# Decode attention over two key/value caches on one core: blocks of 8192 keys by 8 heads, 16 KB runs per load, output weights loaded last

## The chip, the core and the metric

The kernel runs on one core of a Trainium2 chip. The metric is the device time of one execution in microseconds (us), the median of several. The engines' short names in the profile are PE (TensorE; PEld its weight loads), DVE (VectorE), ACT (ScalarE), POOL (GpSimd) and SP (SyncE, which here issues the loads). "DMA engines" are the sixteen engines that move data between HBM and SBUF.

## The reference

Two attention blocks decode one token each. Block A has 32 heads over 32,768 keys, each head with its own cache. Block B has 32 query heads on 8 cache heads and looks only at the last 4096 keys. Everything is bfloat16, head size 128, model width 512.

```python
# A: q = x @ wq -> (1, 32, 1, 128)
scores = jnp.einsum("bhqd,bhkd->bhqk", q, k_cache) * (Dh ** -0.5)
p = _softmax(scores, axis=-1)
o = jnp.einsum("bhqk,bhkd->bhqd", p, v_cache)
out_A = o.transpose(0, 2, 1, 3).reshape(B, Sq, H * Dh) @ wo
# B: the same over k_cache[:, :, Sk-4096:, :], each of 8 cache heads serving 4 query heads
# result: concatenate([out_A, out_B], axis=-1)
```

Both caches are read once: 536.9 MB for A and 16.8 MB for B, and 16.8 MB of weights. That is 570.4 MB in all. Each byte of A's K and V is used for one query only, each byte of B's for four.

## The kernel before

The kernel works in rounds of 2048 keys by all 32 heads (two rounds of B, 16 of A). A load brings 2048 keys of two heads (1 MB). A partition holds 16 neighbouring keys of 128 bfloat16, which is a run of 4 KB in HBM.

```python
ROWS = 2048
def kv_src2(self, name, which, r, kvh0):
    base = d["key0"] + ROWS * r
    ap = d[which][0, kvh0:kvh0 + 2, base:base + ROWS, :]
    return ap.rearrange("s (p j) d -> p s j d", j=JT)          # JT = 16: 4 KB runs
```

In a round, PE transposes each K tile (into PSUM, DVE copies it back), and multiplies it with a query column, so that the scores of all 32 heads end in 128 partitions of one PSUM bank. The softmax follows over the whole bank. The probabilities are then "spread": 32 small matmuls with a 0/1 matrix place them so that they can serve as PE weights, and ACT copies each product back. Only then can the PV matmuls of that round run, while K of the next round arrives:

```python
for uu, unit in enumerate(kunits):                 # 16 K units of a round
    ...                                            # transposes and scores of two heads
    if s == 0 and uu >= self.SPREAD_POS and spreads:
        emit_spreads(j, spreads[:4], sp_first)     # 4 of 32 per unit
    if uu + 1 >= self.PVSTART and not spreads and vi < len(vunits):   # PVSTART = 9
        emit_PV(j, vunits[vi], vi == 0)            # one V unit per K unit
        vi += 1
...
while vi < len(vunits):                            # what is left, in one go
    emit_PV(j, vunits[vi], vi == 0)
```

With eight V buffers and PV starting at the ninth unit, eight of the 16 PV units are left for the round's end. The last loads of the kernel are the output weights of A, in 1 KB runs, and then 16 V units. (The code above is shortened.)

## Time and profile before

The median before was 1474.56 us (1472.97 to 1483.99, 3 runs).

| what | value |
|---|---|
| busy PE / DVE / ACT | 77% / 50% / 21% |
| load queue, share of sixteen engines' time | 98.1% |
| mean rate of HBM reads | 387 GB/s |

These lines come from the page of the kernel before: busy time of the engines, the stretch of 40 slices (DMA in tenths, GB/s), the DMA packets, the load queue (q1), the queue that fetches instructions (q8), and the chain of work that ended last.

```profile
PE 1135.4 (77%) x15670; PEld 774.8 (53%) x15670; DVE 732.5 (50%) x1240; ACT 307.2 (21%) x601; POOL 6.1 (0%) x25
...
DMA  9999999999999999999999999999999999999994
GB/s 353 392 395 403 387 390 409 392 409 408 393 408 375 409 373 408 401 389 358 389 409 373 409 406 377 409 379 408 373 409 396 395 403 392 407 391 409 386 394 160
DMA packets 157360, 572.64 MB, mean 388 GB/s; under 512 B 9761, under 2 KB 17953, under 8 KB 157218
...
q1 hardware_dynamic: 157218, 570.46, 98.1%
q8 instruction: 123, 2.02, 0.6%
...
DMA 51%; PE 33%; SPq 9%; ACT 4%; DVE 1%; issue 1%; ACTq 0%; DVEq 0%
```

A "98.1%" queue looks like a bound that nothing but fewer bytes could move. But the slices swing between 358 and 409 GB/s. The windows view of the kernel before (columns: stretch, its length, then busy time and instruction count of each engine, granted clock of PE, DMA share, GB/s) tells three states apart:

```profile
core 0: us, PE busy (x) PEld busy (x) DVE busy (x) ACT busy (x) POOL busy (x), PEclk, DMA share, GB/s
22.00:24.00 2.00, 0.00 (x0) 0.00 (x0) 0.00 (x0) 0.00 (x0) 0.00 (x0) 1.00 1.06 390
435.00:440.00 5.00, 4.38 (x79) 3.10 (x77) 3.44 (x6) 0.00 (x0) 0.00 (x0) 0.98 1.03 410
455.00:460.00 5.00, 5.00 (x146) 4.37 (x144) 1.16 (x2) 0.00 (x0) 0.00 (x0) 0.93 0.54 167
1405.00:1410.00 5.00, 3.18 (x6) 0.52 (x6) 0.50 (x4) 3.55 (x8) 0.00 (x0) 0.50 1.10 352
1452.00:1454.00 2.00, 1.11 (x16) 0.63 (x16) 0.00 (x0) 0.00 (x0) 0.00 (x0) 0.50 0.40 154
1454.00:1456.00 2.00, 0.92 (x16) 0.63 (x16) 0.00 (x0) 0.00 (x0) 0.00 (x0) 0.50 0.03 12
```

Query weights in 2 KB runs stream at 390 GB/s (row 22), K and V in 4 KB runs at 410 (row 435), output weights in 1 KB runs at 352 (row 1405), each with a DMA share at or above 1. Row 455 is a gap: PE is busy for all 5 us with 146 matmuls, and the engines carry 167 GB/s at a share of 0.54. From about 1453 on nothing moves, and the kernel ends at 1475.3. Who held the loads back is told by the waits of the load queue (L361 is line 361 of the kernel; columns: us waited in total, times, longest):

```profile
SPq L361 <- PE psACC L504: 650.9, 126, 18.3
SPq L352 <- PE psT L432: 139.9, 74, 9.8
```

The loads of V (L361) waited 650.9 us in total for PV matmuls (L504) to set a buffer free. Most of those waits cost nothing, since other loads were in flight; row 455 shows where one did.

### The profile page before, as it was taken

The numbers are of one execution on the slowest core, as the hardware profiler recorded it, in microseconds if no ns is written. First come the engines' busy times: TensorE is split into PE (matmuls) and PEld (weight loads), VectorE is DVE, ScalarE is ACT, GpSimd is POOL, SyncE is SP. The second block draws the span as 40 slices with busy tenths as digits, with TensorE's granted clock in tenths as the row PEclk, the third lists the DMA queues.
The fourth block names the chain that finished last, engine by engine and source line by source line (L and its number), as shares of the span: only waits on it lengthen the run. The fifth ranks groups of instructions, "written<-read, shape, count | busy, mean of one in ns | idle before, by whom it ended". The sixth has DMA issues, their size and how long they took to land.

```text
span 1475.3 us, 34189 instructions
## 1 busy us (share of the span) xinstructions
PE 1135.4 (77%) x15670; PEld 774.8 (53%) x15670; DVE 732.5 (50%) x1240; ACT 307.2 (21%) x601; POOL 6.1 (0%) x25
## 2 busy tenths in 40 slices
PE   2989878687777878878787878777787787878764
PEld 2656565555555455555545555554555555555522
DVE  1567545455454545544454645545455554545403
ACT  0112204040311304031130403113040311304040
POOL 1000000000000000000000000000000000000000
PEclk9799989999998979897998989989899998989956
DMA  9999999999999999999999999999999999999994
GB/s 353 392 395 403 387 390 409 392 409 408 393 408 375 409 373 408 401 389 358 389 409 373 409 406 377 409 379 408 373 409 396 395 403 392 407 391 409 386 394 160
DMA packets 157360, 572.64 MB, mean 388 GB/s; under 512 B 9761, under 2 KB 17953, under 8 KB 157218
## 3 DMA queue, kind: packets, MB, share of 16 engines
q1 hardware_dynamic: 157218, 570.46, 98.1%
q8 instruction: 123, 2.02, 0.6%
q14 instruction: 19, 0.16, 0.0%
HBM read 570.43 MB, written 0.00 MB: 387 GB/s over the span
## 4 chain that ended last, share of the span: by engine, by line
DMA 51%; PE 33%; SPq 9%; ACT 4%; DVE 1%; issue 1%; ACTq 0%; DVEq 0%
DMA kbuf<-in_A_k_cache_dram 47%; PE psT L432 21%; SPq L361 6%; PE psS L455 5%; ACT ptz L849 4%; PE psP L481 3%; PE psACC L504 3%; DMA vbuf<-in_A_v_cache_dram 3%; SPq L352 2%; DMA kbuf<-in_B_k_cache_dram 1%; SPq L326 1%; SPq L341 1%; PE psP L410 0%; DVE kt L682 0%; PE psACC L613 0%
## 5 line engine op out<-in xcount | busy, mean ns | idle before, releaser
L682 DVE COPY kt<-psT 128x1024 bf16<-128x1024 bf16 x1056 | 687.5, 687 | 561.7 <-PE psT L432 553.1
L432 PE MATMUL psT<-ident,kbuf 128*128 128x128 bf16 x8448 | 629.0, 235 | 203.6 <-DMA kbuf<-in_A_k_cache_dram 172.7
L432 PEld LDWEIGHTS psT<-ident,kbuf 128*128 128x128 bf16 x8448 | 538.4, 106 | 328.8 <-DMA kbuf<-in_A_k_cache_dram 211.4
L849 ACT ACTIVATE ptz<-psP 128x512 bf16<-128x512 f32 x512 | 276.6, 594 | 341.6 <-PE psP L481 341.5
L481 PE MATMUL psP<-E_A,psb 32*128 32x512 bf16 x512 | 183.9, 401 | 75.3 <-ACT ptz L849 60.4
L455 PE MATMUL psS<-kt,qzA 128*32 128x512 bf16 x2048 | 214.1, 411 | 0.4 <-DVE kt L682 0.4
L504 PE MATMUL psACC<-vbuf,ptz 128*32 128x256 bf16 x4224 | 172.6, 297 | 47.7 <-DMA vbuf<-in_A_v_cache_dram 45.9
L504 PEld LDWEIGHTS psACC<-vbuf,ptz 128*32 128x32 bf16 x4224 | 143.6, 139 | 71.3 <-DMA vbuf<-in_A_v_cache_dram 53.2
L830 ACT ACTIVATE alpha_A<-m_A,nb 128x1 f32<-128x1 f32 x16 | 4.7, 294 | 702.0 <-DVE nb L694 702.0
L481 PEld LDWEIGHTS psP<-E_A,psb 32*128 32x128 bf16 x512 | 37.9, 92 | 213.2 <-ACT ptz L849 181.9
L455 PEld LDWEIGHTS psS<-kt,qzA 128*32 128x32 bf16 x2048 | 54.2, 94 | 58.6 <-DVE kt L682 13.2
L712 DVE SCALAR_TENSOR_TENSOR o_A<-o_A,alpha_A,psACC 128x256 f32<-128x256 f32 x16 | 7.7, 481 | 152.1 <-PE psACC L504 152.1
L852 ACT ACTIVATE ptz<-psP 128x288 bf16<-128x288 f32 x32 | 11.4, 408 | 24.4 <-PE psP L481 23.7
L690 DVE TENSOR_REDUCE cmax<-psS 128x1 f32<-128x512 f32 x18 | 12.5, 692 | 2.3 <-PE psS L455 0.5
L832 ACT ACTIVATE psb<-psS,nb 128x512 bf16<-128x512 f32 x18 | 12.0, 668 | 0.0
L830 ACT ACTIVATE alpha_B<-m_B,nb 128x1 f32<-128x1 f32 x2 | 0.6, 294 | 52.1 <-DVE nb L694 52.1
L481 PE MATMUL psP<-E_B,psb 32*128 32x288 bf16 x32 | 8.0, 289 | 3.2 <-ACT ptz L852 3.1
L455 PE MATMUL psS<-kt,qzB 128*32 128x512 bf16 x64 | 6.8, 438 | 1.1 <-DVE kt L682 0.8
L481 PEld LDWEIGHTS psP<-E_B,psb 32*128 32x128 bf16 x32 | 2.3, 91 | 9.2 <-ACT ptz L852 7.2
L863 ACT ACTIVATE e_gamma_A<-m_A,e_nb_A 128x1 f32<-128x1 f32 x1 | 0.3, 295 | 31.3 <-DVE e_nb_A L771 31.3
L807 DVE COPY e_part_A<-psACC 1x512 f32<-1x512 f32 x4 | 2.7, 686 | 3.4 <-PE psACC L613 3.4
L644 DVE COPY E_A<-ident 32x16 bf16<-32x16 bf16 x4 | 0.8, 195 | 7.1 <-POOL out_sb L314 7.0
(106 smaller groups left out, 70.3 us busy)
## 6 DMA issues: line engine op xcount, KB each, us to landing
kbuf<-in_A_k_cache_dram SPq DMA_DIRECT2D x256, 1024.0 KB, 12.7
vbuf<-in_A_v_cache_dram SPq DMA_DIRECT2D x256, 1024.0 KB, 13.1
kbuf<-in_B_k_cache_dram SPq DMA_DIRECT2D x8, 1024.0 KB, 13.9
vbuf<-in_B_v_cache_dram SPq DMA_DIRECT2D x8, 1024.0 KB, 13.0
vbuf<-in_B_wq_dram SPq DMA_DIRECT2D x4, 1024.0 KB, 8.8
vbuf<-in_A_wq_dram SPq DMA_DIRECT2D x4, 1024.0 KB, 14.5
wob<-in_B_wo_dram SPq DMA_DIRECT2D x4, 1024.0 KB, 13.7
kbuf<-in_A_wo_dram SPq DMA_DIRECT2D x4, 1024.0 KB, 12.0
```

The lines of the kernel that those rows point to most:

```text
L326: e.dma_start(self.wq_view(ch), src).then_inc(self.vfull[slot], 16)
L341: e.dma_start(self.wo_view(ch), src).then_inc(sem, 16)
L352: e.dma_start(self.K_buf[slot][:, :, :, :], src).then_inc(self.kfull[slot], 16)
L361: e.dma_start(self.V_buf[slot][:, :, :, :], src).then_inc(self.vfull[slot], 16)
L432: inst = t.transpose(self.T[tb][:, 128 * jjj:128 * (jjj + 1)], self.K_buf[kslot][:, s, j, :], self.ident[:, :])
L455: inst = t.matmul(self.S[sb_][32 * c:32 * c + 32, :], lhsT=win, rhs=self.KT[ktslot][:, 512 * c:512 * (c + 1)], start=(hh == 0), stop=(hh = ...
L481: inst = t.matmul(out_ap, lhsT=lhsT, rhs=rhs, start=True, stop=True, tile_position=(32 * c, 0))
L504: inst = t.matmul(self.ACC[32 * c:32 * c + 32, 0:2 * DH], lhsT=self.pt_window_unit(name, c, jj, win_u), rhs=self.V_buf[vslot][:, 0:2, tile ...
L682: inst = v.tensor_copy(self.KT[ktslot][:, 1024 * half:1024 * (half + 1)], self.T[tb][:, :])
L690: seq(v.reduce_max(self.cmax[:, :], self.S[j % 2][:, :], axis=AXX))
L832: s.activation(out=self.p_sb[j % 2][:, :], in_=self.S[j % 2][:, :], func=ACTF.Exp, bias=self.nb[:, :], scale=self.SCALE, accum_out=self.ro ...
L849: inst = s.activation(out=tz[:, 512 * half:512 * (half + 1)], in_=self.P[pb][:, 0:512], func=ACTF.Copy)
```

## The change

The intent is to keep the DMA engines streaming in long runs. The kernel is rewritten; this is a shortened cut of the diff, with comments in place of what is left out:

```diff
-ROWS = 2048
-        ap = d[which][0, kvh0:kvh0 + 2, base:base + ROWS, :]
-        return ap.rearrange("s (p j) d -> p s j d", j=JT)
+        a["KC"], b["KC"] = 4, 2
+            d["HG"] = 32 // d["KC"]                # 8 heads of A at a time, 16 of B
+            d["blk"] = 2048 * d["KC"]              # 8192 keys of A, 4096 of B
+        ap = d[which][0, h0:h0 + nh, base:base + d["blk"], :]
+        return ap.rearrange("s (p j) d -> p s (j d)", p=128)   # 16 KB runs (A), 8 KB (B)
 ...
-        # 32 spreading matmuls and 32 ACT copies per round
+        for jj in range(4):                        # probabilities transposed whole
+            inst = e.transpose(PT[:, 128*jj:128*jj+128], pb[:, 128*jj:128*jj+128], ident)
+        # one ACT copy per round
 ...
+                    if i > 0 and pr == 1 and u % 2 == 1 and pv_done < dp["nvu"]:
+                        self.emit_PV(i - 1, pv_done)   # one 4 MB V unit after every 2nd K unit
 ...
-        src = X[name]["wo"][1024*k:1024*(k+1), :].rearrange("(a p) c -> p a c", p=128)
+        src = self.X[name]["wo"].rearrange("(p a) c -> p (a c)", a=32)   # 32 KB a row
+            if u == d["nvu"] - 1:                  # after the last V unit
+                for part in range(3):
+                    self.load_wo("A", part)
```

Loads are 2 MB instead of 1 MB. There are four K buffers of 2 MB and three V buffers of 4 MB. The counts of transposes, score matmuls and PV matmuls hardly change.

## The prediction

> **What bounds the kernel now.** DMA. The page gives PE 77%, DVE 50%, ACT 21% busy of 1475.3 us; the load queue's packets fill 98.1% of sixteen engines, 570.46 MB, and the chain of waits is 51% DMA. Three losses stand out in the windows view:
>
> 1. *Rate by run length.* While streaming, output weights (1 KB runs) move at 352 GB/s, query weights (2 KB) at 387 to 390, K and V (4 KB) at 409 flat. This fits about 8.7 ns per run plus 0.037 ns per byte on each of 16 engines (an estimate from these rates).
> 2. *A gap per round.* At the end of A rounds the rate falls for about 5 us (455 to 460: 167 GB/s; 540 to 545: 139) while PE is 100% busy with a burst of delayed PV matmuls, which hold the V buffers (load queue's waits: 650.9 us on the PV line).
> 3. *Ends.* Bytes start at 3.9 us; after the last byte (about 1453) 22 us of end chain run.
>
> Check: 553.6 MB at 409 + 8.4 at 388 + 8.4 at 352 = 1398 us; bytes flow over 1449 us, so 51 us are gaps, 3.2 us a round.
>
> **The change.** Same bytes. Runs become 16 KB (A caches, weights) and 8 KB (B caches). By the fit: 427 GB/s at 16 KB, 421 at 8 KB: A 536.9 MB 1258 us, B 40, weights 40: 1338 us.[...] no run yet shows 16 KB.
>
> The spreading matmuls (183.9 + 8.0 us PE) and their ACT copies (276.6 + 11.4 us) go, replaced by 4 transposes and one copy a round: off the path themselves, but they delayed PV. PV now runs evenly, one unit after every second K load; transposes, scores and PV (629 + 221 + 173 us) keep their counts, so PE needs about 1025 us of 1350, DVE 740. With 8 MB of K and 12 MB of V buffers, loads are about 25 us ahead; a round's softmax chain of some 4 us should no longer reach the queue. I expect 0 to 8 us of gaps left.
>
> End: after the last V come 9.8 us of output weights. Meanwhile run PV (4 us at the 0.5 clock the trace shows there), merge and normalise (3.5 us), then 32 one-row projection matmuls serially, 216 to 427 ns each ([...]the trace agrees: 32 in four column groups took 3.52 us), about 9 us, copy 0.7, store about 2. So some 10 us remain after the last byte, not 22.
>
> **Sum.** 3.9 + 1338 + 10 + about 3 = **1355 us**, ratio 0.92. Range 1342 to 1390. Chances: faster 0.97, same 0.02, slower 0.01.
>
> **What would show it.** Packets near 40,000 instead of 157,218; mid-run windows at 427 GB/s; no window under 380 between 20 and 1340 us; waits on K and V as PE's main idle; 8 to 13 us after the last byte.
>
> **What would make it wrong.** If the hardware cuts runs to 4 KB, the rate stays 409 and the time is about 1410.[...] If half-clock stretches make PE the pace, gaps return.[...]

The 216 and 427 ns behind the "about 9 us" of the projection are in the trace of the kernel before: the matmuls over 512 columns of its output projection (L613), in groups of four, begin 0.427 us apart while the granted clock is 0.50 and 0.216 us apart once it is 1.00.

## The result

The changed kernel takes 1366.76 us (1365.49 to 1367.88, 4 runs) against 1476.05 us before (4 runs). The ratio is 0.9249 (95% interval 0.9215 to 0.9284). The result was correct. These are the same lines of the page of the kernel after:

```profile
PE 951.6 (70%) x15172; PEld 734.7 (54%) x15172; DVE 767.8 (56%) x1414; ACT 29.9 (2%) x73; POOL 2.4 (0%) x11
...
DMA  9999999999999999999999999999999999999995
GB/s 392 422 425 426 427 426 427 427 425 427 425 426 427 426 426 427 425 426 427 427 424 427 425 427 427 425 426 426 427 426 425 426 426 428 426 426 425 426 405 213
DMA packets 40762, 572.51 MB, mean 419 GB/s; under 512 B 4659, under 2 KB 4661, under 8 KB 4789
...
q1 hardware_dynamic: 40340, 570.44, 98.5%
q8 instruction: 119, 1.95, 0.6%
...
DMA 77%; PE 20%; DVE 1%; issue 1%; SPq 0%; ACT 0%
```

There are 40,340 packets in the load queue instead of 157,218, and the slices stand at 424 to 428 GB/s from the third to the thirty-eighth. The last two are 405 and 213. The windows view of the kernel after (columns as before) shows that end:

```profile
600.00:605.00 5.00, 5.00 (x82) 3.57 (x84) 3.59 (x6) 0.00 (x0) 0.00 (x0) 0.75 1.02 429
1300.00:1302.00 2.00, 2.00 (x49) 1.54 (x50) 2.00 (x4) 0.00 (x0) 0.00 (x0) 1.00 0.64 262
1302.00:1304.00 2.00, 1.70 (x56) 1.09 (x44) 0.77 (x3) 0.00 (x0) 0.00 (x0) 1.00 0.56 238
1334.00:1336.00 2.00, 2.00 (x44) 1.35 (x40) 0.00 (x0) 0.00 (x0) 0.00 (x0) 0.50 0.99 420
1338.00:1340.00 2.00, 2.00 (x11) 0.81 (x10) 0.18 (x1) 0.00 (x0) 0.00 (x0) 1.00 0.81 334
1346.00:1348.00 2.00, 0.00 (x0) 0.00 (x0) 0.00 (x0) 0.00 (x0) 0.00 (x0) 0.66 0.52 221
1354.00:1356.00 2.00, 1.54 (x4) 0.49 (x5) 0.28 (x2) 0.00 (x0) 0.00 (x0) 0.50 0.45 188
1358.00:1360.00 2.00, 2.00 (x11) 0.79 (x10) 0.00 (x0) 0.00 (x0) 0.00 (x0) 1.00 0.00 0
```

Full rate lasts until 1336, but for one gap from 1300 to 1304 us (262 and 238 GB/s): the next loads of V were issued only at 1303.3, when PV had freed their buffer. From 1340 on, for about 18 us, the DMA share is near 0.5 and the rate near half, and only at about 1358 does the last byte land. That was not foreseen. Halves are a hint: eight of the sixteen engines had finished, eight had not. The trace has sixteen increments of each load's semaphore, at up to sixteen times. They are read here as one per engine as its part lands; the windows fit that reading, with a DMA share of 0.52 and 0.45 (1346 and 1354) when eight increments of the last load were in (by 1345.2 us) and eight were not. Worked out from them, the spread between the first and the last engine of one load, at several moments of the kernel after:

```
load complete at us   engines' landings, us before the last one
   109.8   -3.3 -3.3 -3.3 -3.2 -3.0 -2.9 -2.3 -1.9   -1.8 -1.8 -1.7 -1.6 -1.6 -1.6 -1.6 0
   657.2  -12.8 -12.6 -12.5 -12.4 -12.3 -11.8 -11.0 -6.8   -1.9 -1.9 -1.9 -1.8 -1.7 -1.6 -0.2 0
  1314.0  -23.7 -23.5 -23.3 -23.3 -23.2 -21.9 -21.5 -12.8   -2.2 -2.0 -2.0 -1.9 -0.4 -0.3 -0.1 0
  1357.9  -18.5 -18.5 -18.3 -18.2 -18.2 -18.2 -17.9 -12.7   -2.2 -0.4 -0.4 -0.4 -0.3 -0.2 -0.1 0
```

Seven engines and, less far, an eighth run ahead of the other eight, by about 1.7 us more per 100 us. The lead grows in steps of about 1.56 us. In the gap at 1300 us it fell by 4.9 us, from 23.7 to 18.8: the DMA share was 0.64 and 0.56 there, which fits that the early engines had run out of issued loads while the late ones went on. In the kernel before, the spread stayed under 3 us throughout. Between two of its gaps (466 to 532 us) the mean lead of the earlier eight landings over the later eight grew from 0.5 to 1.5 us, and after the next gap it was 0.4 again: there too, each gap let the late ones catch up. The timeline of the kernel after, from the landing of the last V (1348.1) on, in three of its lines (start, length, engine, line, what):

```profile
1348.20 3.59 PE L525 MATMUL psACC<-vbuf,ptsb 128*8 128x256 bf16 x64 [4.43 <-issue]
...
1354.46 8.25 PE L583 MATMUL psS<-kbuf,oz_A 128*1 128x512 bf16 x32 [0.62 <-DVE oz_A L572]
...
1362.75 0.68 DVE L588 CAST out_sb<-psS 1x512 bf16<-1x512 f32 x1 [8.44 <-PE psS L583]
```

PV takes 3.59 us, the merge until 1354.46, the projection 8.25 us, and the copy of the result 0.68 us.

### The profile page after: what moved, and what is told of

Same layout as the page of the kernel before. It is cut to its first block, busy times and chain, and to the rows that moved or that the text cites. A ratio compares the mean times of both kernels' runs of the same rounds, so it can differ in the third digit from the quotient of the medians. Undisturbed runs are those within 1.5% of the kernel's fastest.

```text
span 1365.0 us, 32343 instructions
## 1 busy us (share of the span) xinstructions
PE 951.6 (70%) x15172; PEld 734.7 (54%) x15172; DVE 767.8 (56%) x1414; ACT 29.9 (2%) x73; POOL 2.4 (0%) x11
## 2 busy tenths in 40 slices
DMA packets 40762, 572.51 MB, mean 419 GB/s; under 512 B 4659, under 2 KB 4661, under 8 KB 4789
## 3 DMA queue, kind: packets, MB, share of 16 engines
q1 hardware_dynamic: 40340, 570.44, 98.5%
## 4 chain that ended last, share of the span: by engine, by line
DMA 77%; PE 20%; DVE 1%; issue 1%; SPq 0%; ACT 0%
DMA kbuf<-in_A_k_cache_dram 73%; PE psT L417 15%; PE psS L444 3%; DMA kbuf<-in_B_k_cache_dram 3%; DMA vbuf<-in_A_v_cache_dram 2%; PE psS L583 1%; PE psACC L525 1%; DVE kt L421 0%; SPq L203 0%; DVE oc_B L551 0%; PE psPT L565 0%; ACT psb L472 0%; DVE o_B L535 0%; DVE tr_in L460 0%; DVE nbg_B L491 0%
## 5 line engine op out<-in xcount | busy, mean ns | idle before, releaser
L421 DVE COPY kt<-psT 128x1024 bf16<-128x1024 bf16 x1056 | 672.5, 685 | 427.0 <-PE psT L417 423.7
L417 PE MATMUL psT<-ident,kbuf 128*128 128x128 bf16 x8448 | 641.3, 243 | 361.2 <-DMA kbuf<-in_A_k_cache_dram 294.9
L417 PEld LDWEIGHTS psT<-ident,kbuf 128*128 128x128 bf16 x8448 | 577.5, 111 | 489.8 <-DMA kbuf<-in_A_k_cache_dram 335.6
L444 PE MATMUL psS<-kt,qz_A 128*32 128x512 bf16 x2048 | 177.2, 427 | 0.0
L525 PE MATMUL psACC<-vbuf,ptsb 128*8 128x256 bf16 (+1 forms) x4160 | 132.9, 283 | 23.9 <-issue 21.7
L525 PEld LDWEIGHTS psACC<-vbuf,ptsb 128*8 128x8 bf16 (+1 forms) x4160 | 103.0, 89 | 55.2 <-issue 23.4
L537 DVE SCALAR_TENSOR_TENSOR o_A<-o_A,alpha_A,psACC 128x256 f32<-128x256 f32 x48 | 23.1, 480 | 87.5 <-PE psACC L525 87.5
L444 PEld LDWEIGHTS psS<-kt,qz_A 128*32 128x32 bf16 x2048 | 32.1, 97 | 31.5 <-issue 10.4
L472 ACT ACTIVATE psb<-psS,nb_A 128x512 bf16<-128x512 f32 x16 | 11.0, 687 | 1157.8 <-DVE nb_A L470 1157.8
L503 PEld LDWEIGHTS psPT<-ident,psb 128*128 128x128 bf16 x72 | 5.7, 123 | 15.3 <-issue 11.8
L460 DVE TENSOR_REDUCE tr_in<-psS 128x1 f32<-128x512 f32 x18 | 12.2, 680 | 0.0
L395 PE MATMUL psACC<-x_B,vbuf 128*128 128x1 bf16 x128 | 3.7, 165 | 11.5 <-DMA x_B<-in_B_x_dram 10.9
L395 PEld LDWEIGHTS psACC<-x_B,vbuf 128*128 128x128 bf16 x128 | 3.6, 104 | 11.6 <-DMA x_B<-in_B_x_dram 10.9
## 6 DMA issues: line engine op xcount, KB each, us to landing
kbuf<-in_A_k_cache_dram SPq DMA_DIRECT2D x128, 2048.0 KB, 33.8
vbuf<-in_A_v_cache_dram SPq DMA_DIRECT2D x128, 2048.0 KB, 38.4
```

The lines of the kernel that those rows point to most:

```text
L395: inst = e.matmul(ps[:, h:h + 1], lhsT=wq[:, 4096 * tt + 128 * h:4096 * tt + 128 * h + 128], rhs=t["x"][:, tt:tt + 1], start=(tt == 0 and ...
L417: inst = e.transpose(T[:, 128 * k:128 * k + 128], self.kbuf[slot][:, DH * tile:DH * tile + DH], self.ident[:, :])
L421: self.tcopy.append(self.op("dve", lambda v, T=T, KT=KT: v.tensor_copy(KT[:, :], T[:, :]), o, self.sread.get(b - self.NKT)))
L444: inst = e.matmul(bank[32 * c:32 * c + 32, :], lhsT=t["qz"][:, off:off + 32], rhs=self.kt[(b0 + c // 2) % self.NKT][:, 512 * (c % 2):512 * ...
L460: o = dve(lambda v: v.reduce_max(tr["in"][:, 0:1], self.S[i % 2][:, :], axis=AXX), sdone)
L472: e = self.op("act", lambda s: s.activation(out=pb[:, :], in_=self.S[i % 2][:, :], func=ACTF.Exp, bias=t["nb"][:, r:r + 1], scale=self.SCA ...
```

## The experiments

The main theory says that the gain is the sum of three things (longer runs, no gaps, a shorter end), and that a new cost appears: the fetches of PE's instructions go through eight of the sixteen DMA engines and hold those up. The rivals are named with each run. Three runs, marked "on one chip", were made to tell a few microseconds apart. The other differences from the changed kernel compare different chips; it took 1366.76 us in its first runs and 1366.81 on that one chip.

### 1. Short runs again (a_4kA)

```diff
-        return ap.rearrange("s (p j) d -> p s (j d)", p=128)
+        # A only: the same 8192 keys as four groups of 2048, so 4 KB per run
+        return ap.rearrange("s (q p j) d -> p (s q) (j d)", p=128, j=16)
```

The result stays right, because softmax and sum do not care which partition holds a key, as long as K and V agree.

> The changed kernel with the A caches' loads cut into 4 KB runs (94% of all bytes; same 2 MB loads and order of work; only which keys a partition holds differs). Theory run length: packets of 4 KB take 161 ns against 613 ns for 16 KB, so those 537 MB stream at 409 and not 427 GB/s and the time rises by about 54 us, to 1420 (1410 to 1430). Rival: the gain of rate came from the 2 MB loads and the deeper queue, not the runs: time stays within 15 us of 1366.

It took 1422.39 us (1420.19 to 1422.76). Two lines of its page, slices and packets:

```profile
GB/s 393 416 404 408 408 408 408 408 408 408 408 408 409 408 409 409 409 408 399 410 408 405 406 409 403 409 401 410 409 395 408 407 403 409 406 400 407 403 413 259
DMA packets 139065, 572.51 MB, mean 403 GB/s; under 512 B 4658, under 2 KB 4660, under 8 KB 135860
```

The rate is 408 to 409 in most slices, as in the kernel before, with 2 MB loads and the new order of work. So run length, not load size, set the rate, and it is worth 55.6 us for A's caches alone. The packets' durations in the traces agree: the median is 613 ns for 16 KB, 312 for 8 KB, 161 for 4 KB. One thing is open: the lag of the late engines stopped growing at about 11 us here (11.5 at the last load, not 18.5), though 119 blocks of instructions were fetched as before. (A first form of this kernel, a_4k, with B's caches cut too, did not build: "Unable to balance aps with more than 3 dims".)

### 2. The gaps of the kernel before (b_pv)

```diff
-                if uu + 1 >= self.PVSTART and not spreads and vi < len(vunits):
+                while (uu + 1 >= self.PVSTART and not spreads and vi < len(vunits)
+                       and vi <= min(2 * (uu + 1 - self.PVSTART) + 1, uu - 2)):
                     emit_PV(j, vunits[vi], vi == 0)
```

> The kernel before with one change: from the ninth K unit of a round on, two PV units per K unit (no more than have landed) in place of one, so that about 2 and not 8 are left for a burst at the round's end. Theory gap: the burst holds the V buffers and starves the queue; the windows near round ends no longer fall to 140 to 170 GB/s and the time falls by 20 to 40 us, to 1435 to 1455; a part of the 51 us of gaps, some 20 us, is the engines' unequal pace by instruction fetches and stays. Rival: the gap comes from the softmax chain at the round's end: time within 8 us of 1475.

It took 1449.19 us (1447.23 to 1451.4) against 1478.15 before on the same chip, 29 us less; the ratio is 0.9807 (0.978 to 0.9835). The windows of this run at the places where the kernel before had its gaps:

```profile
455.00:460.00 5.00, 2.16 (x52) 1.40 (x41) 1.49 (x4) 0.03 (x1) 0.00 (x0) 0.95 1.03 408
...
540.00:545.00 5.00, 2.92 (x34) 2.44 (x35) 2.18 (x5) 0.96 (x3) 0.00 (x0) 0.50 1.02 408
```

408 GB/s stands where 167 and 139 stood. The softmax chain at the round's end is unchanged in this kernel, so it was not the cause of these gaps. The burst of PV was, and it is worth 29 of the 51 us that the prediction counts as gaps.

### 3. Fewer PE instructions (a_fewT)

```diff
-                for k in range(8):
+                for k in (range(8) if b < 8 else (0,)):
```

This uses stale keys on purpose, so it is not a valid kernel. (The check of the output with these inputs does not tell such an error.) All loads stay.

> The changed kernel with 7 of 8 transposes left out once the buffers have been filled once (wrong result on purpose). Loads are the same. Theory fetch: PE's instruction stream shares the DMA engines, about 1.55 us per 16 KB block on one of eight engines; PE instructions fall from 30.3 to about 15.6 thousand, blocks from 119 to about 62, so the late half of the engines lags 10 us at the end and not 19, and the time falls by about 9 us, to 1357 (1353 to 1360). Rival: eight engines are slower by their place (memory or port), whatever PE does: lag 19 us, time 1364 to 1367.

It took 1355.87 us (1355.39 to 1356.68), 10.9 us less than the changed kernel, as the theory of fetches expects. Its page's lines for PE and for the instruction queue:

```profile
PE 723.0 (53%) x7836; PEld 286.6 (21%) x7836; DVE 740.2 (55%) x1414; ACT 29.9 (2%) x73; POOL 2.4 (0%) x11
...
q8 instruction: 62, 1.02, 0.3%
```

62 blocks (packets of the instruction queue, 16,384 B each in the changed kernel's trace) are fetched instead of 119, and in the last load seven engines lead by 11 to 13 us, not 18 (landings before the last one: 13.0 12.9 12.9 12.5 12.4 11.9 11.4, and the other nine from 2.2 to 0). The eighth engine, which lies between the groups in the changed kernel, is with the late ones here and with the early ones in a run below (17.0 us); why is open. A slowness that belongs to the engines' place should have left the lag alone. It shrank with the fetches: at the same load near the end (landing at 1303.7 us here and at 1314.0 in the changed kernel) the seven lead by 11.5 to 13.0 us against 21.5 to 23.7, which is 0.53 to 0.55 of it, and 62 blocks are 0.52 of 119. PE's granted clock was 0.58 here and 0.85 in the changed kernel, and the slices show the same 425 to 430 GB/s in mid-run.

### 4. More PE instructions (a_more, a_more2, and again on one chip)

```diff
+                for _ in range(4):                 # a_more2: only from the 400th batch on
+                    e.transpose(T[:, 0:1], self.kbuf[slot][0:1, 0:DH], self.ident[0:1, 0:1])
                 for k in range(8):
```

Each added transpose reads one row of K and is overwritten at once, so it adds instructions and hardly any data.

> The changed kernel with four tiny extra transposes of one row ahead of each batch of eight (overwritten by the batch; result unchanged): 4224 matmuls, so about 8450 PE instructions or 33 more blocks of 16 KB to fetch. Theory fetch: the late half of the engines lags about 4 x 1.5 = 6 us more, and the time rises by 6 us, to 1372 (1370 to 1375). Rival, the saving in the run with fewer transposes came from PE having less to do: PE stays under 90% busy here, so the time stays at 1366.

It took 1390.34 us, 18 us more than expected. The slices of its page show why:

```profile
GB/s 393 421 284 368 427 426 425 424 427 427 426 424 427 425 426 424 427 425 426 425 426 426 426 425 426 425 427 425 427 422 426 422 424 423 424 423 418 424 392 199
```

In the third and fourth slice (34.7 us each) the rate is 284 and 368: PE had fallen behind there (windows of it show PE busy throughout from 80 to 90 us at a granted clock of 0.59, and again from 105 to 135), and the loads waited for K buffers. Against 427 those two slices lost 11.6 + 4.8 = 16.4 us. The 7 us that remain of the 23.6 us fit the 6 us of the fetches, but this run alone cannot say so: the rival had PE keep up, and here it did not. So the additions were moved past that stretch.

> As the run with tiny extra transposes, but only from the 400th batch on, past the stretch where PE had fallen behind: 2624 more matmuls, 20 more 16 KB blocks of instructions, 2.6 per fetching engine at 1.53 us. Theory fetch: about 4 us more than the changed kernel, 1370.7 (1369 to 1373), with no window under 400 GB/s in mid-run. Rival, instructions cost only what PE needs: 1366 to 1367.

It took 1371.57 us (1371.26 to 1372.5).

> The changed kernel unaltered, on the chip of the next two runs, so that differences of a few us can be told: 1366 to 1368 on every theory.

> The late extra transposes (2624 matmuls, 20 more blocks of PE instructions) beside the changed kernel on one chip. Theory fetch: 4 to 5 us slower than it, ranges apart. Rival, instructions cost only what PE needs: no difference.

On one chip, the unaltered kernel took 1366.81 us (1365.91 to 1367.53) and this one 1371.45 us (1370.11 to 1371.93): the ranges do not meet. These are the slices and the instruction queue of that second run's page:

```profile
GB/s 392 422 414 423 427 426 427 426 426 427 425 427 426 425 426 426 426 426 425 427 426 425 425 426 426 425 426 425 427 424 425 426 427 425 423 419 419 421 399 219
...
q8 instruction: 140, 2.29, 0.7%
```

There are 140 blocks, and the rate stays at or above 414 from the second to the thirty-eighth slice. The last four of these dip to 419 to 423, lower than in the changed kernel: the early engines' lead had passed 23 us and stopped growing at 25, which fits that they ran out of issued loads. So the lag at the last load is no larger than in the unaltered kernel (17.9 us in both), against what was expected; but that load lands 4.8 us later (1363.6 against 1358.7), enough for the whole difference in time. With 21 more blocks, 2.6 per engine if there are eight, 4.6 us is 1.8 us a block on its engine; the run with fewer transposes gives 10.9 / (57 / 8) = 1.5 us a block; the steps of the lead, 1.56 us. PE was busy for 79% of the span, so it did not set the pace.

| run | 16 KB blocks of instructions | time us | difference to the changed kernel |
|---|---|---|---|
| a_fewT | 62 | 1355.87 | -10.9 |
| changed | 119 | 1366.76 | |
| a_more2 (two chips) | 139, 140 | 1371.57, 1371.45 | +4.8, +4.6 |

### 5. The order of the last loads (a_wofirst)

```diff
+            if u == d["nvu"] - 1:
+                for part in range(3):
+                    self.load_wo("A", part)
             self.load_v(last, u, 0)
             self.load_v(last, u, 1)
-            ... (the three loads of A's output weights stood here)
```

> The changed kernel with the order of its last loads undone: A's output weights are loaded before the last V unit, not after. Theory: the last V then lands about 9.8 us later (1358), and the chain of 17 us behind it (PV, merge, projection, store) follows whole: 1375 (1372 to 1378). Rival: the last load of either kind sets the end, the order is worth under 3 us.

It took 1376.83 us (1375.59 to 1377.97), 10.1 us more. In its timeline the last PV starts at 1358.21 us, not at 1348.20, and from there to the end of the span it takes 17.1 us against 16.8. So the chain behind the last V sets the end, and 9.8 us of weights were hidden beside it.

### 6. An attempt to even out the two halves (a_wob8, a_wob8s): failed

The author assumed that a load of 8 partitions runs on 8 of the engines, the same ones each time. If those were the eight that are early, B's output weights could go through them alone.

```diff
+        rows = 8 if name == "B" else 128
+        for p0 in range(0, 128, rows):
+            self.load(dst[p0:p0 + rows, :], src[p0:p0 + rows, 512*a0:512*a1], self.wosem[name][part], ...)
```

> The changed kernel with the B output weights (4 MB) loaded by 32 loads of 8 partitions each, which should use only 8 of the 16 DMA engines. Theory fetch: if these 8 are the engines without instruction fetches, the slow half is relieved of 9.8 us, both halves end together near 1348 and the time falls by 8 to 10 us, to 1356 to 1358. If they are the fetching ones, their lag doubles and the time rises by about 10 us, to 1375 to 1378. Rival, the halves' lag has no cost: time within 3 us of 1366.

> As the run with the B output weights on 8 engines, but each load's 8 partitions are 4 apart and not neighbours. If the 37 us lost there came from 8 engines writing into 8 neighbouring partitions at once, that loss goes and only the balance is left: 1356 to 1358 if the 8 engines are those without fetches, about 1376 if they are those with them. If it came from many small loads clogging the issuing queue, the time stays near 1400.

They took 1403.69 and 1394.31 us, both worse than either branch of the theory allowed; the second lies nearest to its rival, the clogged queue. That each of these loads used 8 engines is borne out: the packets under 512 B rose by 223 to 4,882, and 32 loads of 8 increments less 2 loads of 16 are 224. (In the changed kernel 4,403 of the 4,659 such packets are of 4 bytes, and its trace has 4,404 increments by loads.) That they were the same 8 was not shown. But in the last V of a_wob8s twelve engines landed within 9 us of each other (34.7 to 25.8 us before the last one) and four far behind (17.9, 9.9, 4.0 and 0 us before it). This suggests, but does not show, that the eight engines used do not all belong to the early ones. One that does not would carry 0.5 MB of these weights instead of 0.25 MB, an estimated 9.8 us more at the mean rate of one engine (427 / 16 GB/s), and so explain about 10 us of the loss. The loads also clogged their own queue, as the timeline of SP in a_wob8s shows (16 loads in one line, of 22 us):

```profile
1303.57 21.98 SPq L203 DMA_DIRECT2D kbuf<-in_B_wo_dram  x16
1325.59 4.69 SPq L203 DMA_DIRECT2D vbuf<-in_A_v_cache_dram  x2
```

In the changed kernel, one load of the same weights took 0.43 us to issue. Spreading each load's partitions won back 9 of the 37 us. The cause of the loss stays open, above all of the 18 us or so beyond those 10, and so does a way to give the late half less.

### 7. A shorter last step (a_tail, a_tail_b)

```diff
-   inst = e.matmul(bank[0:1, 0:512], lhsT=oz[:, a:a+1], rhs=self.wo_at(name, a), start=(a == 0), stop=(a == 31))
+   c = a % 4
+   inst = e.matmul(bank[32*c:32*c+1, 0:512], lhsT=oz[:, a:a+1], rhs=self.wo_at(name, a),
+                   start=(a < 4), stop=(a > 27), tile_position=(0, 32 * c))
+   # then one copy of the bank to SBUF and one matmul with a 0/1 column adds the four rows
```

> The changed kernel with its last step shortened: the 32 one-row projection matmuls go in turn to four column groups, and one copy and one matmul add the four rows. The chain after the last V is what ends the kernel: the 8.3 us of projection after the normalisation become about 3.1 to 4.1 (until the last weights have landed) plus 1.7 us to add up: 3 to 4 us less, 1363 (1361 to 1365). Rival, the last load's landing sets the end: no change.

> The shortened last step once more, its four partial rows added in bfloat16: in the first form the float32 add-up matmul took 1.86 us at the half clock, in bfloat16 it should take about 0.45. So 1.4 us less than that form and about 2.6 us less than the changed kernel beside it: 1364 (1363 to 1365), the least that the last weights' landing at 1358 leaves.

They took 1365.53 us and, on one chip with the changed kernel's 1366.81, 1364.65 us (1363.99 to 1365.57). The first fell short of the 3 to 4 us expected, because the step that adds the rows was mis-sized, as two lines of its timeline show (the copy and the matmul):

```profile
1359.02 0.69 DVE L590 COPY part<-psS 128x512 f32<-128x512 f32 x1 [4.28 <-PE psS L585]
...
1359.76 1.86 PE L591 MATMUL psS<-part,e 128*1 128x512 f32 x2 [0.80 <-DVE part L590]
```

In float32 the adding matmul (two instructions) took 1.86 us at the half clock, against 1.02 us for the same form at a granted clock of 1.00 in the kernel before (L621), and in bfloat16 (a_tail_b) 0.59. In both, the second half of the projection waited for weights, the last of which landed at 1358.3 and 1359.1. The landing of the late half therefore sets a floor, and 2.2 us is what this idea is worth. a_tail_b is the fastest valid version found, but only by 0.2%; a_tail itself, run on another chip than the changed kernel, cannot be told from it (1365.27 to 1365.77 against 1365.49 to 1367.88).

## Why the prediction was right

The range (1342 to 1390) held the time, and the direction and size were right: 1355 predicted, 1366.8 measured, 11.8 us apart. The range is 48 us wide, and it was this width that took in a cost nobody had foreseen; there the prediction was lucky. Point by point:

- **Rate by run length: right.** The fit from three rates gave 427 GB/s at 16 KB; the windows show 426 to 429, and a packet took 613 ns where the fit gives 615. The fixed cost per run was the estimate from those three rates, and the packets bear it out: a median of 48 ns for 1 KB, 87 for 2 KB and 161 for 4 KB in the kernel before. From 100 to 1300 us the changed kernel's mean rate was 426. Taking the long runs away cost 55.6 us (54 expected).
- **Gaps: the cause was right, the size only in part.** The burst of PV cost 29 us, measured in the kernel before. The prediction put all 51 us down to it and had them vanish to "about 3". The rest was not taken apart. Part of it are dips that b_pv still has (352 GB/s in its window 415 to 420). Part may be the late engines: 123 blocks at 1.5 us over eight engines are an estimated 23 us for each of them, and half of that against the mean rate of all sixteen, on which the 51 us rest; no run tested this.
- **The step that failed** is the term "about 3" for what is left of gaps. With it the sum puts the last byte at 1345 us; it landed at 1357.9, 13 us later. In its place stands the lag of the late eight engines, 18.5 us at the last load. Seven engines landed their last bytes by 1340.0 us, near the 1342 that the sum's first two terms give, an eighth at 1345.2, and the late half by 1357.9. Experiments 3 and 4 show that this lag comes from the fetches of PE's instructions, which the sum had no term for. A sum of bytes over a rate gives the mean engine's finish, and a load is complete only when the slowest of sixteen has landed.
- **Lead of the loads: right, with an effect not thought of.** Loads of A landed a median of 33.8 us (K) and 38.4 us (V) after their issue, against 12.7 and 13.1 before, and no round's softmax chain shows as a gap between the third slice and 1300 us. This lead also let the early engines run 23 us ahead, so that the lag, which the gaps of the kernel before kept under 3 us, was paid at the end.
- **The end: right in its steps.** In the span 7.1 us followed the last byte (1357.9 to 1365.0), and 8.8 us in the device time, which is 1.7 us longer; 10 were predicted and 8 to 13 allowed. From the last V on it was 16.8 us, where the prediction's steps add up to about 19. PV took 3.59 us (4 predicted) and the projection 8.25 (9). The projection's matmuls began 0.43 us apart while the granted clock was 0.50, and 0.216 us apart from 1356.9 on, when it was 1.00. "No window under 380 between 20 and 1340" failed twice: in its last 2 us (334), and in the gap at 1300 to 1304 us (262 and 238).
- **Busy time of PE: nearly right.** 951.6 us against "about 1025", 70% of the span. PE's main idle was the wait for K, as said.

The three measured parts, 55.6 (runs of A), 29 (gaps) and 10.1 (order of the last loads), add up to 94.7 of the 109.3 us between the two medians; two were measured by undoing a part in the changed kernel and one by doing it in the kernel before, so that they need not add up exactly. The rest was not tested by itself. By the rates of section "Time and profile before", the weights' longer runs make an estimated 6 us of it (8.4 MB at 352 and 8.4 at 390 instead of 427). The chain after the landing of the last V is also shorter (16.9 us, against 20.3 from 1455.0 to 1475.3 before), but what that is worth was not measured.

## What to carry to other kernels

When loads are the bound, read the rate per run length from windows of the kernel's own trace, fit a cost per run, and check the fit with one run that changes the run length alone. Count the PE instructions as traffic: a stream of 30,344 of them (15,172 matmuls and as many weight loads) put half of the DMA engines up to 23.8 us behind the others here, and the deep queue of this kernel moved most of that loss to the end. When the DMA share falls to one half, look at the sixteen landings of a load rather than at its completion.

## What the traces show of instruction fetches, run length and small loads

- The instruction queue (q8) moves packets of 16,384 B: 119 of them in the changed kernel for 30,344 PE instructions, 62 for 15,672 in a_fewT, 140 for 35,592 in a_more2_again, so 253 to 255 instructions a block. In this kernel, bound by its loads, the fetches were not hidden: 57 blocks fewer gained 10.9 us, 21 more lost 4.6 us, an estimated 1.5 to 1.8 us of one of eight DMA engines per block.
- The trace does not number the engines. The signs that these fetches use eight of the sixteen are that eight fall behind and eight do not, and that the fetches' durations in the changed kernel repeat with a period of eight: 1016 1026 1073 1078 1058 1099 1100 1095, then 1018 1018 1073 1068 1060 1100 1100 1087 ns. A third sign is in the landings: seven fetches began at 648.3, 655.7, 668.0, 683.7, 690.4, 705.1 and 711.1 us, and in the loads complete at 652.4, 662.1, 671.9, 686.6, 696.4, 711.1 and 716.0 one more increment of the late half came about 1.6 us later each time, while the lead of the early half stood still. Which engines they are is open.
- For SyncE's queue the run length decided the rate and the size of the load did not: 352 GB/s at 1 KB, 390 at 2 KB, 409 at 4 KB in 1 MB and in 2 MB loads, 427 at 16 KB.
- Loads over few partitions had a price: 32 loads of 8 partitions in place of two of 128 made the kernel 28 to 37 us longer, and sixteen of them took 22 us to issue in a_wob8s, where one load of the same weights took 0.43 us in the changed kernel.
